# Three buffers instead of four for the transposed unit vectors of a pair of heads, from batch 3 on

## The chip, the core and the metric

The kernel runs on one core of a Trainium2 chip. The metric is device time in microseconds (us) of one execution, the median of several runs. TensorE (PE) does the matrix products, VectorE (DVE) and ScalarE (ACT) move and transform what it leaves in its eight banks, GpSimd (POOL) issues the loads of inputs and weights, SyncE (SP) issues stores and the loads of intermediate results.

## What is computed

Attention with unit queries and keys, followed by a mixer and a two-layer perceptron:

```python
q_n = q / (np.linalg.norm(q, axis=-1, keepdims=True) + 1e-06)
k_n = k / (np.linalg.norm(k, axis=-1, keepdims=True) + 1e-06)
attn = softmax(np.matmul(q_n, k_n.transpose(0, 1, 3, 2)) / tau)
x = np.matmul(attn, v)                 # 8 batches, 12 heads, 448 rows, 64 wide
h = x.transpose(0, 2, 1) @ U @ V       # mixes rows through rank 32
u = x + h.transpose(0, 2, 1)           # 8 x 448 x 768
out = u + np.maximum(u @ w_ch1, 0.0) @ w_ch2     # 768 -> 3072 -> 768
```

## The kernel before

**Two halves that share PE.** Attention goes batch by batch and, in a batch, by six pairs of heads. The perceptron goes over 28 tiles of 128 tokens: a first group of three and one single tile, then twelve groups ("hosts") of two. Hosts 0 to 5 do their first layer at L1299 and their second, in seven products instead of eight, at L1328. Hosts 6 to 11, which run after attention, use seven products for both layers (L1192 and L1328). While attention runs, perceptron products fill PE wherever attention's next step isn't ready.

**Who sets the order.** Everything is first recorded as operations with an engine, a planned duration, dependencies, and slots of buffer rings that it takes and gives back. A planner (`Plan.run`) then walks through planned time and fixes the order of instructions on every engine. An operation that needs a slot is not placed before the planner believes the slot free. Some operations (squares, copies, relus) may go to ACT or DVE, whichever is free first in the plan. On the chip each engine runs its list strictly in order.

**The life of a pair.** The q and k of two pairs are loaded together by POOL (L596). Squares (ACT L657 or DVE L661), their sums (DVE L665), root and inverse (ACT L679 and L680, DVE L685 and L687), and two scalings (DVE L733) give the unit vectors of a pair, `xn`. From batch 2 on eight PE transposes (L574 from `qk_all`, "the flip of the pair") put them into a bank and one copy (ACT L1475 or DVE L1477, `sqk<-bank`) into a tile of the ring `r_qkT`. That tile is what the change is about. The scores of three (pair, key chunk) slots at a time are one burst of matmuls (L797), seven bursts to a batch from batch 2 on. The exponentials are ACT L815, the product with V is L842, its scaling DVE L873 and L874. A tile of `r_qkT` comes free when the last burst that reads its pair is done. Because the last 64 keys of two pairs share a slot, burst 2 reads pairs 1, 2 and 3, and burst 4 reads pairs 3, 4 and 5.

**The ring.** `r_qkT` is a `Shrink`: six tiles for the first 18 pairs (`NPAIR * WHOLE`, three batches), and then only those listed in `left`, in turn. The other tiles' memory passes to the perceptron's weight sums (`T4` at L1107 lies over tiles 0 and 1), once `r_gone2` says that they are free.

**After a batch.** Its result X is projected (L959), expanded again (L1012) and added (DVE L1021). Each token tile of 128 rows is then stored by SP (L1050, `u<-X_sb`, 192 KB), turned by six PE transposes (L574 from `X_sb`), copied back over X in place by ACT L1475 or DVE L1477 (`X_sb<-bank`), and stored turned (L1060). The in-place copy may not start before the L1050 store has read X, so it waits for that store's landing. V of a batch is loaded by POOL with eleven transfers (L619, L624), right behind the batch's last load of q and k in POOL's list.

**The other rings of this path.** `r_xn` holds two pairs from batch 3 on and `r_ld` two loads of two pairs. A pair is scaled only after the flip two pairs earlier, and a load of q and k starts only after the scalings two loads earlier. So a flip that comes later makes the scalings, the loads and the V loads behind them come later.

Of the kernel before, what the change touches and what calls it, by code (L numbers as in the profile page):

```python
# [317 lines left out]
def kernel(  # L318
# [18 lines left out]
    NPAIR = H // 2  # L337
# [14 lines left out]
    WHOLE = 3  # L352
# [21 lines left out]
    def fixed_ring(tiles):  # L374
# [6 lines left out]
            for i in range(3)]  # L381
# [13 lines left out]
    r_inv = ring(4, [SCH, 2, G, SC], FP, "inv")  # L395
    qkT_t = sqk_t[:, 3 * SQ:]
    r_qkT = Shrink([qkT_t[:, 2 * SC * SCH * i:2 * SC * SCH * (i + 1)].rearrange("p (b s) -> p b s", b=2 * SC)
                    for i in range(6)], NPAIR * WHOLE, (2, 3, 4, 5))
    X_t = const.tile([128, 2 * 4 * C], BF, name="X_sb")
    r_X = fixed_ring([X_t[:, 4 * C * i:4 * C * (i + 1)].rearrange("p (t c) -> p t c", t=4) for i in range(2)])  # L400
    A_t = const.tile([128, 3, C], BF, name="A_sb")
# [1288 lines left out]
```

## Time and profile before

| what | value |
|---|---|
| median of 3 runs | 572.73 us (572.58 to 574.4) |
| the profiled execution | 573.77 us, of which its span 572.0 us |
| PE busy | 561.3 us (98%), 6721 matmuls |
| DVE busy | 464.3 us (81%) |
| ACT busy | 306.2 us (54%) |
| POOL busy | 148.5 us (26%) |
| granted PE clock | 1.000 |
| last score burst starts | 381.9 us |

Busy time is a sum over the whole span. The text below reads three more views: windows of ten microseconds, which give each engine's busy time in a stretch; the waits, which say who waited for whom; and the timeline, where a row gives start, length, engine, line, operation, output and input, count, and in brackets the idle time before it with its releaser.

### The profile page before, as it was taken

To read this page: it belongs to the slowest core of one execution; us is meant where nothing else is said; L and a number is where in the kernel's file an instruction comes from. 1 tells how busy PE (TensorE), PEld (TensorE's weight loads), DVE (VectorE), ACT (ScalarE), POOL (GpSimd) and SP (SyncE) were. 2 spreads that over 40 slices of the span, in tenths; PEclk is the share of its full clock that TensorE was granted. 3 is DMA by queue.
4 is the path that set the end of the run, shared out by engine and by line. 5 is a ranking of instruction groups with operands and counts; after the bars stand their busy time and mean duration, and the time that the engine had idled before them with its cause. 6 is when DMAs were issued, how large, how long until landed. Compare 5 with 4: busy or idle time off the path is not lost.

```text
span 572.0 us, 16131 instructions
## 1 busy us (share of the span) xinstructions
PE 561.3 (98%) x6721; PEld 412.7 (72%) x6722; DVE 464.3 (81%) x1061; ACT 306.2 (54%) x495; POOL 148.5 (26%) x180
## 2 busy tenths in 40 slices
PE   8899999999999999999999999999999999999996
PEld 6565656768767758767867766876969696969784
DVE  8979859999898989979969976687897776758583
ACT  7977655766567874766865684560404141414140
POOL 8526241002424225124120510001030303030302
PEclk9999999999999999999999999999999999999999
DMA  9999997632968849349645922312124121221201
GB/s 156 204 207 139 210 192 107 144 84 52 105 155 128 87 88 177 64 93 136 95 83 101 131 70 71 112 30 84 30 78 127 37 83 31 83 69 45 79 7 55
DMA packets 116264, 57.61 MB, mean 101 GB/s; under 512 B 72256, under 2 KB 116192, under 8 KB 116192
## 3 DMA queue, kind: packets, MB, share of 16 engines
q0 software_dynamic: 72352, 25.73, 39.8%
q1 hardware_dynamic: 43840, 30.87, 18.8%
q8 instruction: 52, 0.85, 0.6%
q14 instruction: 20, 0.16, 0.1%
HBM read 61.65 MB, written 20.64 MB: 144 GB/s over the span
## 4 chain that ended last, share of the span: by engine, by line
PE 91%; DVE 5%; ACT 1%; DMA 1%; issue 1%; POOL 0%; SPq 0%; DVEq 0%; POOLq 0%
PE bank L1328 28%; PE bank L1299 16%; PE bank L1192 15%; PE bank L842 8%; PE bank L797 6%; PE bank L1411 6%; PE bank L1453 6%; PE bank L574 5%; DVE qk_all L733 2%; PE bank L1012 1%; DVE ss L665 1%; PE bank L959 1%; DMA relu<-in_k_dram 1%; DVE X_sb L1021 0%; DMA out_dram<-relu 0%
## 5 line engine op out<-in xcount | busy, mean ns | idle before, releaser
L815 ACT ACTIVATE attn<-bank 128x896 bf16<-128x896 f32 (+1 forms) x163 | 140.1, 915 | 35.8 <-PE bank L797 35.3
L1328 PEld LDWEIGHTS <-relu 128*128 128x128 bf16 x1008 | 95.5, 98 | 66.2 <-issue 7.7
L1299 PE MATMUL bank<-uT,w_sb 128*128 128x256 bf16 x864 | 106.1, 273 | 1.6 <-ACT relu L1309 1.4
L1328 PE MATMUL bank<-w_sb,relu 128*128 128x384 bf16 x576 | 103.4, 326 | 0.0
L1299 PEld LDWEIGHTS <-w_sb 128*128 128x128 bf16 x864 | 81.0, 98 | 20.3 <-issue 9.9
L665 DVE TENSOR_REDUCE ss<-sqk 112x8 f32<-112x512 bf16 x95 | 62.1, 675 | 3.1 <-ACT sqk L657 2.6
L733 DVE TENSOR_TENSOR qk_all<-qk_all,inv 112x512 bf16<-112x512 bf16 x93 | 60.5, 683 | 0.3
L842 PE MATMUL bank<-v_nat,attn 128*128 128x65 bf16 (+1 forms) x1536 | 58.3, 193 | 0.8 <-DVE X_sb L880 0.6
L842 PEld LDWEIGHTS <-attn 128*128 128x128 bf16 (+1 forms) x1536 | 53.8, 97 | 5.4 <-issue 3.3
L596 POOL DMA_DIRECT2D qk_all<-in_q_dram x24 | 17.7, 738 | 147.9 <-ACT attn L815 49.1
L1309 ACT ACTIVATE relu<-bank 128x512 bf16<-128x512 f32 x48 | 28.7, 598 | 44.1 <-PE bank L1299 43.3
L1192 PEld LDWEIGHTS <-w_sb 128*128 128x128 bf16 x864 | 49.3, 98 | 0.8
L797 PE MATMUL bank<-sqk 64*64 64x448 bf16 (+1 forms) x460 | 46.9, 356 | 0.7 <-ACT sqk L1475 0.5
L1229 ACT COPY attn<-bank 128x512 f32<-128x512 f32 x18 | 10.6, 587 | 65.6 <-PE bank L1192 60.6
L1220 ACT ACTIVATE relu<-relu 128x512 bf16<-128x512 bf16 x36 | 22.7, 630 | 29.7 <-DVE relu L1214 28.8
L1192 PE MATMUL bank<-uT,w_sb 128*128 128x128 bf16 x648 | 38.1, 219 | 0.0
L1353 POOL TENSOR_TENSOR relu<-relu,u_nat 128x384 f32<-128x384 f32 x7 | 8.4, 1205 | 110.0 <-ACT relu L1351 82.7
L1411 PE MATMUL bank<-uT,w_sb 128*128 128x384 bf16 (+1 forms) x288 | 35.6, 273 | 0.0
L619 POOL DMA_DIRECT2D v_nat<-in_v_dram x42 | 31.1, 746 | 17.2 <-DMA w_sb<-in_moe_w_ch_dram 14.6
L1453 PE MATMUL bank<-w_sb,relu 128*128 128x384 bf16 x192 | 35.4, 326 | 0.0
L874 DVE TENSOR_TENSOR X_sb<-bank,rd 128x256 bf16<-128x256 f32 x72 | 30.6, 425 | 2.6 <-DVE rd L873 0.2
L1353 POOL TENSOR_TENSOR attn<-attn,u_nat 128x384 f32<-128x384 f32 x6 | 12.8, 2156 | 69.0 <-ACT attn L1351 69.0
(137 smaller groups left out, 943.2 us busy)
## 6 DMA issues: line engine op xcount, KB each, us to landing
qk_all<-in_q_dram POOLq DMA_DIRECT2D x23, 224.0 KB, 4.2
qk_all<-in_k_dram POOLq DMA_DIRECT2D x23, 224.0 KB, 5.5
u_nat<-u SPq DMA_DIRECT2D x25, 192.0 KB, 2.5
w_sb<-in_moe_w_ch_dram POOLq DMA_DIRECT2D x4, 1152.0 KB, 17.9
w_sb<-in_moe_w_ch_dram POOLq DMA_DIRECT2D x8, 576.0 KB, 15.5
uT<-uT SPq DMA_DIRECT2D x24, 192.0 KB, 3.0
u<-X_sb SPq DMA_DIRECT2D x22, 192.0 KB, 2.0
uT<-X_sb SPq DMA_DIRECT2D x21, 192.0 KB, 3.1
```

What stands on the lines that cost most here:

```text
L619: ops = [load(lambda j=j, r0=r0, c=c, s0=s0, s1=s1: nc.gpsimd.dma_start(out=v_t[b % 2][r0:r0 + s1 - s0, :, j, 0:D], in_=src[c, s0:s1]), (s ...
L665: lambda i=i, a0=a0, a1=a1, sq=sq: nc.vector.reduce_sum(ss.tile[:, i, a0:a1, :].rearrange("p h c -> p (h c)"), sq.tile[:, 0:a1 - a0, :].re ...
L733: (nc.gpsimd if pool_ else nc.vector).tensor_mul(dst, src, sc)
L797: nc.tensor.matmul(out=out, lhsT=qkT.tile.rearrange("p b s -> p (b s)")[r, n0:n0 + w], rhs=qkT.tile[r, SC:2 * SC, :].rearrange("p c s -> p ...
L815: exps.append(plan.add(Op("ACT", act_t(2 * S, 0.058), lambda sc=sc, c=c, attn=attn: nc.scalar.activation(out=attn.tile[:, :, off:off + S] ...
L842: nc.tensor.matmul(out=av.tile[:, t, 0:D + 1], lhsT=tail.tile[:, hh, 128 * t:128 * (t + 1)] if tail and j == SC - 1 else (attn if j < SC - ...
L874: nc.vector.tensor_mul(X.tile[:, :, h * D:(h + 1) * D], av.tile[:, :, 0:D], rd.tile.to_broadcast([128, 4, D]))
L1192: o = plan.add(Op("PE", pe_t(128), lambda i=i, j=j, jj=jj: nc.tensor.matmul(out=mm.tile[:, 128 * jj:128 * jj + 128], lhsT=left[k](i, j), r ...
L1299: o = plan.add(Op("PE", pe_t(256), lambda j=j, e=e, cc=cc, mm=mm: nc.tensor.matmul(out=mm.tile[:, 256 * e:256 * e + 256], lhsT=w1_sb[:, cc ...
L1328: o = plan.add(Op("PE", pe_t(CH), lambda j=j: nc.tensor.matmul(out=mm.tile[:, 0:CH], lhsT=left[k](j), rhs=right[k](j), start=(first and j ...
L1411: o = plan.add(Op("PE", pe_t(n), lambda cc=cc: nc.tensor.matmul(out=mm.tile[:, m:m + n], lhsT=w1_sb[:, cc, f * 128:(f + 1) * 128], rhs=uT. ...
L1453: nc.tensor.matmul(out=mm.tile[:, 0:c1 - c0], lhsT=relu.tile[:, f, i * 128:(i + 1) * 128], rhs=w2_t[:, f, c0:c1], start=(f == 0), stop=(f ...
```

## The change

The ring of the transposed unit vectors keeps three tiles instead of four after its first 18 pairs:

```diff
     r_qkT = Shrink([qkT_t[:, 2 * SC * SCH * i:2 * SC * SCH * (i + 1)].rearrange("p (b s) -> p b s", b=2 * SC)
-                    for i in range(6)], NPAIR * WHOLE, (2, 3, 4, 5))
+                    for i in range(6)], NPAIR * WHOLE, (3, 4, 5))
```

Pair n now takes over the tile of pair n - 3, where it took that of pair n - 4. Tile 2 joins those that `r_gone2` waits for. No instruction is added or removed; the planner lays all of them out anew with the narrower ring.

## Prediction

> **What bounds the kernel.** I read the page's shares first, then the waits of PE, then windows, then the timeline around the one wait that mattered.
>
> ```profile
> PE 561.3 (98%) x6721; PEld 412.7 (72%) x6722; DVE 464.3 (81%) x1061; ACT 306.2 (54%) x495; POOL 148.5 (26%) x180
> ...
> PE 91%; DVE 5%; ACT 1%; DMA 1%; issue 1%; POOL 0%; SPq 0%; DVEq 0%; POOLq 0%
> ```
>
> PE is the bound: 98% busy, 91% of the chain of waits. From 30 to 560 us the windows of ten microseconds show it at 9.8 to 10.0, with one exception, 8.62 between 320 and 330. The waits of PE from 25 to 400 us are 2.6 us in all, and the longest is
>
> ```profile
> PE bank L1299 <- ACT relu L1309: 1.4, 1, 1.4
> ```
>
> (us in total, times, longest). So the change can gain little more than these 2.6 us, 0.45% of the time, and can lose whatever new waits it makes. Is that one wait touched? The timeline of the four engines around it:
>
> ```profile
> 315.75 0.70 POOL L596 DMA_DIRECT2D qk_all<-in_q_dram  x1 [14.69 <-ACT relu L1309]
> ...
> 317.14 4.43 POOL L619 DMA_DIRECT2D v_nat<-in_v_dram  x6
> ...
> 321.56 0.33 SPq L1050 DMA_DIRECT2D u<-X_sb  x1
> ...
> 328.59 0.80 ACT L1475 COPY X_sb<-bank 128x768 bf16<-128x768 bf16 x1 [3.40 <-PE bank L1299]
> 329.29 0.60 ACT L1309 ACTIVATE relu<-bank 128x512 bf16<-128x512 f32 x1
> ...
> 329.94 0.31 PEld L1299 LDWEIGHTS <-w_sb 128*128 128x128 bf16 x3 [1.56 <-issue]
> ```
>
> The releaser named for the copy at 328.59 had long been done. The entry for its line shows ACT's sequencer held before it, and the entry for the store of 321.56 shows why:
>
> ```profile
> L1475 ACTq EVENT_SEMAPHORE  x1: 5512/5512/5512, 323.0 to 323.0; - x1
> ```
> ```profile
> DMA to landing us min/median/max: 7.0/7.0/7.0
> ```
>
> That store took 7.0 us to land where the median of all L1050 is 2.1, because it was issued among the V loads of batch 7. The in-place copy waited for it, the relu behind the copy waited, and PE ran out of banks. From the store's issue to PE's restart are 329.94 - 321.56 = 8.38 us; PE lost 1.56.
>
> **The change, part by part.** *The ring itself* removes no work: both programs have the same number of PE rows, and the order of the two, compared engine by engine, is identical up to the flip of batch 3's fourth pair (near 155 us). The wider `r_gone2` costs nothing: the sums that lie over tiles 0 and 1 (L1117 into `sqk`, 124 us) stand before that point, unmoved. *Flips* move back by one burst: pair 5 of batches 3 to 7 is flipped after burst 3 instead of burst 2, and most others likewise. The shortest cover left between a flip and the burst that reads it is that of batch 3's pair 3: 15 L1328 and some transposes, about 2.8 us, against a copy of 0.62 (DVE) or 0.91 us (ACT). Elsewhere a product with V (32 L842) lies between as well. Cost 0; without that cover it would be about 1 us each. *End of attention*: the last product with V stands 9 matmuls earlier than before, among filler; from host 6 on PE is busy without a break in both. Cost 0.
>
> *POOL's queue.* A later flip makes the scaling (L733) two pairs on later, this the load of q and k, and this the V loads behind it in POOL's list. In the new order the three V runs for batches 5, 6 and 7 stand 150, 160 and 85 matmuls later. Against SP's stores this means:
> - The stores of tile 5 (batches 3 and 5) now precede the load of q by 10 matmuls or more, at least one L733 (0.68 us). Such a place exists before: the store of 314.62, 1.1 us ahead of the load at 315.75, landed in 1.9. So the 1.56 us wait **goes: -1.56**, and behind it nothing else is late: ACT's next L815 follow from bursts that PE itself starts. The store of tile 3 of batch 4 has one L733 between it and its q load too: 0.
> - Site A, about 240 us: the store of tile 6 of batch 3 now lies inside the V run for batch 5, about 5.4 us behind its q load (before: 5.8 behind), and its copy is on ACT with an L1309 behind it.
> - Site B, about 335 us: the same for tile 6 of batch 5, about 6.6 us behind the q load of the V run for batch 7.
>
> What each costs: PE's own time from the store to the matmul that needs the relu, by the timeline (17 L1299 in 1.87 us, 0.11 each; a burst 0.77 with its switch; flip 0.40; L842 0.03 each; X flip 0.34). A: 8 L1299 0.88 + burst 0.77 + 17 L1299 1.87 + flip 0.40 + 32 L842 0.96 + X flip 0.34 + 16 L1299 1.76 = 6.98. B has 7 and 15 L1299: 6.76. With the row's 8.38 us, A waits 8.38 - 6.98 = **1.40** and B 1.62. B's store comes later in the run, though: all V loads had landed at 329.4, 13.6 us behind the q load, so B may see less; a latency of 6.1 gives 0.8. I take **1.2** (0.8 to 1.6). Queued behind each copy on ACT: one L1309, then the three L815 of the next burst, which PE needs only some 20 matmuls later.
>
> Here the Trainium skill reads otherwise. "DMA: Bandwidth & Descriptors", section on the anatomy of one DMA, prices a transfer at 2.0 us plus bytes over 436e3 per us: 2.45 us for 192 KB. With that the copies at A and B find their store landed (the transposes end 4.4 us after it), both cost nothing, and the sum is -1.56. The row says 7.0 in a V run and 1.9 to 2.1 outside it. I follow the row, since both new sites are inside a run[...].
>
> *Banks after burst 3 of batch 4* (site C, near 222 us). In the new order an X flip follows directly on this burst; a L1299 four matmuls later takes the bank that DVE's in-place copy frees. DVE stands before that copy with L874, L1346, L1021, L685, L687, twice L733: 0.43 + 0.56 + 0.55 + 0.17 + 0.35 + 1.37 = 3.4 us, plus 0.17 (L873) and the copy 0.5, so 4.1 against PE's 3.9. The wait is 0.2 if DVE comes to it on time and 1.3 if it is a microsecond late, as its load just before allows (from burst 2 to burst 3 the new order holds 12.6 us of DVE work beside 11.6 of PE, each instruction at its row's mean). **0.7** (0 to 1.3).
>
> **Sum:** -1.56 + 1.40 + 1.2 + 0.7 = +1.7 us. The profiled execution (span 572.0, 1.8 around it, 573.8) would become 575.5; it lies 1.0 above the median shown, so the median becomes 572.73 + 1.74 = **574.5**.
>
> **Rivals.** *R1, the stores land in time.* If issue to landing stays under 5.5 us at A and B, they cost nothing, C closes, and the old wait is gone: 572.73 - 1.56 = **571.2**, faster. For it: stores at 317.65 and 319.92 in the same run landed in 6.0 and 4.6, so it isn't always 7. Against: six L1050 stores inside the V runs near 217 and 265 us belong to the same kind of traffic, and the maximum of the line is 7.0. It decides at 5.5 us.
>
> *R2, DVE becomes the bound.* The planner gives DVE 9 more squares (0.417), 3 relus (0.688), 2 `A_sb` copies and one `X_sb` copy (0.55), and 2 `sqk` copies (0.616) fewer: 3.75 + 2.06 + 1.65 - 1.23 = 6.2 us more, and ACT 7.4 less. DVE's rests before are
>
> ```profile
> 240.00:250.00 10.00, 10.00 (x109) 6.49 (x108) 5.73 (x15) 7.18 (x10) 2.66 (x3) 1.00 0.33 61
> 290.00:300.00 10.00, 10.00 (x103) 5.91 (x102) 4.57 (x12) 6.71 (x10) 3.03 (x4) 1.00 0.25 61
> ```
>
> (the fifth figure: 5.73 and 4.57 us of ten). In the new order the stretches between bursts 6 and 0 hold 4.3 us of DVE work where 2.4 stood (batch 4) and 5.5 where 1.1 stood (batch 5), beside some 4 to 5 us of PE. DVE would reach the next relus (L1311) late. If half of the 6.2 us ends in PE waits, with the collisions at 1.0 net: 572.73 + 3.1 + 1.0 = **576.8**. Against: DVE was 95% or more busy in several windows before, and PE waited for it 0.8 us in all from 25 to 400 us.
>
> *R3, one wait for another.* A takes the place of the old wait, B and C hide: 572.73 - 1.56 + 1.4 = **572.6**. For it: the waits near 217 and 265 us before, with stores as late, cost PE nothing since filler was there.
>
> That the ring isn't full, so that nothing moves, is excluded: the flips move.
>
> **Chances.** What a measurement of this kernel tells from no change is about 0.3%, 1.7 us. The forecast has 0.40 (its own range 573.4 to 575.8, 0.6 of it beyond the bound), R1 0.15 (two thirds of it faster by more than the bound, if small waits of PE go too), R2 0.25, R3 0.20. Slower: 0.24 + 0.25 + 0.01 = 0.50; faster 0.11; same 0.39. Half of R1 and the upper part of R2 stay outside the range: 571.5 to 577.3.
>
> **What would show it.** Right: no wait of PE near 328 us; two waits of PE for ACT's L1309, 1 to 1.6 us, near 240 and 335, each with an in-place X copy ahead of it whose store took 6 to 7 us; one of 0.2 to 1.3 for DVE's L1477 near 222. R1: L1050 at no more than about 5 us in the runs, and no such waits. R2: PE waits for L1311 or `sqk` copies of DVE, DVE near 10 of 10 at 240 to 250 and 290 to 300 with no late store. Wrong altogether: a PE wait at a burst (L797) for a flip's copy, or a longer stretch after 400 us, where I expect the same 174 us.

## The result and the profile after

The changed kernel takes **572.38 us** in the median of 20 runs (571.77 to 573.37), the kernel before, run beside it, 573.81 (572.58 to 574.97). The ratio is 0.9977 with a 95% interval of 0.9969 to 0.9984: about 1.3 us faster (1.43 between the medians), where 1.7 slower was forecast. The forecast started from a median of three runs, 572.73; beside the changed kernel that kernel's median is 1.1 higher, so what follows compares differences and not the 574.5 with the 572.38. The profiled execution takes 571.8 us, its span 570.0 (before: 573.8 and 572.0).

The page's shares of busy time and of the chain of waits, of the kernel after:

```profile
PE 559.8 (98%) x6721; PEld 411.9 (72%) x6722; DVE 469.4 (82%) x1074; ACT 300.9 (53%) x482; POOL 148.8 (26%) x180
...
PE 92%; DVE 3%; DMA 2%; POOL 1%; issue 1%; ACT 0%; DVEq 0%; POOLq 0%; ACTq 0%
```

DVE has 13 instructions and 5.1 us more, ACT 13 and 5.3 us fewer: the count is the prediction's, the times are below its 6.2 and 7.4. PE is the bound as before. The waits of PE from 25 to 400 us, after:

```profile
PE bank L842 <- DVE X_sb L880: 0.6, 2, 0.4
PE bank L1328 <- ACT relu L1309: 0.3, 1, 0.3
PE bank L1012 <- issue: 0.2, 1, 0.2
```

The wait of 1.4 us before L1299 is gone. In its place stands one of 0.3 before L1328. It is site B of the prediction, at 333.5 us. The timeline there:

```profile
327.05 0.32 SPq L1050 DMA_DIRECT2D u<-X_sb  x1
...
332.71 0.80 ACT L1475 COPY X_sb<-bank 128x768 bf16<-128x768 bf16 x1 [0.91 <-DMA u<-X_sb]
333.40 1.09 ACT L1309 ACTIVATE relu<-bank 128x512 bf16<-128x512 f32 x2
...
334.06 0.32 PE L1328 MATMUL bank<-w_sb,relu 128*128 128x384 bf16 x1 [0.25 <-ACT relu L1309]
```

The bracket of the copy now names the store itself. Store, copy, relu, matmul: this is the forecast chain with a shorter first link, since the store landed at 332.64, after 5.59 us. Site A, at 236 us:

```profile
227.06 0.70 POOL L596 DMA_DIRECT2D qk_all<-in_q_dram  x1 [18.21 <-ACT relu L1309]
...
231.74 0.32 SPq L1050 DMA_DIRECT2D u<-X_sb  x1
...
236.57 0.80 ACT L1475 COPY X_sb<-bank 128x768 bf16<-128x768 bf16 x1 [1.17 <-PE bank L842]
237.32 0.60 ACT L1309 ACTIVATE relu<-bank 128x512 bf16<-128x512 f32 x1
```
```profile
DMA to landing us min/median/max: 4.8/4.8/4.8
```

The store is issued 4.7 us behind the load of q, the copy does wait for its landing at 236.50 and the relu follows at once, but PE hasn't come to need it. The cost is 0. Site C is in the same trace, 2 us earlier than expected:

```profile
218.79 1.29 DVE L733 TENSOR_TENSOR qk_all<-qk_all,inv 112x512 bf16<-112x512 bf16 x2
218.99 0.74 PE L797 MATMUL bank<-sqk 64*128 64x448 bf16 x6
...
219.67 0.51 PE L574 MATMUL bank<-ident,X_sb 128*128 128x128 bf16 x6
...
220.27 0.36 DVE L1477 COPY X_sb<-bank 128x384 bf16<-128x384 bf16 x1 [0.18 <-issue]
```

DVE was through its two L733 when the X flip ended, so it came on time, and the starts of two L1299 at 220.3 lie 0.23 us further apart than they should: the lower value of the prediction's two (0.2, and 1.3 for a late DVE).

Small waits do not all appear in the list. So I also took the distance between the starts of consecutive matmuls and subtracted the median distance of their shape; bursts and projections aside, where the same distances stand in both, places above 0.12 us from 120 to 400 us are:

| place | before | after |
|---|---|---|
| old wait, 328 us | 1.55 | - |
| site A, B, C | - | 0, 0.42, 0.23 |
| load of `uT` (L908), 173 us | 0.19 | - |
| small ones of before (162.9, 216.4, 231.2, 316.9, 368.7 us) | 1.12 | - |
| small one of after (222.6 us) | - | 0.26 |
| sum | 2.86 | 0.91 |

The difference, 1.95 us, is the 2.0 by which the spans differ. Three fifths are the old wait less B; the rest is small waits, of which the prediction treated only C. The small ones are no accident of one execution: taken in the same way, those of before come to 1.10 to 1.12 us in each of its three profiled executions, and C and the one of after to 0.23 and 0.26 in each of its four.

### The profile page after: what moved, and what is told of

It is laid out like the page before. It is cut to its first block, busy times and chain, and to the rows that moved or that the text cites. A ratio compares the mean times of both kernels' runs of the same rounds, so it can differ in the third digit from the quotient of the medians.

```text
span 570.0 us, 16134 instructions
## 1 busy us (share of the span) xinstructions
PE 559.8 (98%) x6721; PEld 411.9 (72%) x6722; DVE 469.4 (82%) x1074; ACT 300.9 (53%) x482; POOL 148.8 (26%) x180
## 4 chain that ended last, share of the span: by engine, by line
PE 92%; DVE 3%; DMA 2%; POOL 1%; issue 1%; ACT 0%; DVEq 0%; POOLq 0%; ACTq 0%
PE bank L1328 29%; PE bank L1299 16%; PE bank L1192 15%; PE bank L842 8%; PE bank L797 6%; PE bank L1411 6%; PE bank L1453 6%; PE bank L574 4%; PE bank L1012 2%; DMA qk_all<-in_k_dram 1%; DMA u<-X_sb 1%; DVE qk_all L733 1%; PE bank L959 1%; DVE ss L665 1%; POOL qk_all L596 0%
## 5 line engine op out<-in xcount | busy, mean ns | idle before, releaser
L1328 PEld LDWEIGHTS <-relu 128*128 128x128 bf16 x1008 | 95.5, 98 | 65.0 <-issue 6.7
L1299 PE MATMUL bank<-uT,w_sb 128*128 128x256 bf16 x864 | 104.5, 273 | 0.1
L1328 PE MATMUL bank<-w_sb,relu 128*128 128x384 bf16 x576 | 103.7, 326 | 0.3 <-ACT relu L1309 0.3
L1299 PEld LDWEIGHTS <-w_sb 128*128 128x128 bf16 x864 | 81.4, 98 | 18.6 <-issue 8.6
L733 DVE TENSOR_TENSOR qk_all<-qk_all,inv 112x512 bf16<-112x512 bf16 x93 | 60.8, 681 | 0.2
L1309 ACT ACTIVATE relu<-bank 128x512 bf16<-128x512 f32 x45 | 26.8, 597 | 47.6 <-PE bank L1299 46.6
L1353 POOL TENSOR_TENSOR relu<-relu,u_nat 128x384 f32<-128x384 f32 x7 | 9.0, 1289 | 92.8 <-ACT relu L1351 66.3
L1353 POOL TENSOR_TENSOR attn<-attn,u_nat 128x384 f32<-128x384 f32 x6 | 12.8, 2154 | 69.1 <-ACT attn L1351 69.1
```

The lines of the kernel that those rows point to most:

```text
L733: (nc.gpsimd if pool_ else nc.vector).tensor_mul(dst, src, sc)
L1299: o = plan.add(Op("PE", pe_t(256), lambda j=j, e=e, cc=cc, mm=mm: nc.tensor.matmul(out=mm.tile[:, 256 * e:256 * e + 256], lhsT=w1_sb[:, cc ...
L1328: o = plan.add(Op("PE", pe_t(CH), lambda j=j: nc.tensor.matmul(out=mm.tile[:, 0:CH], lhsT=left[k](j), rhs=right[k](j), start=(first and j ...
```

## The experiments

Theories on record: **T1**, the gain is the in-place copy that no longer waits for a late store; **T2**, it is the squares, relus and copies that went from ACT to DVE; **T3**, it is PE's other order. Within T1, on what makes a store in a V run late: **N**, the number of 192 KB stores in flight; **V**, the V loads alone. Ratios are to the kernel before run on the same chip.

### Taking the V loads away

```diff
     order = plan.run()
+    for o in got[7, 0, "v"]:
+        o.fn = lambda: None
```

Before, without the V loads of batch 7:

> The kernel before without the eleven V loads of batch 7 (left out of the computation: batch 7's products use V of batch 5, which is still in that buffer); nothing else moves. T1 (the late landing of the store of 321.56 inside that V run makes the wait of 1.56 us): the store lands in 1.9 to 2.6 us, the copy (L1475) and the relu behind it start when their banks are ready, no PE wait near 328 us, time -1.5 us (ratio 0.9973). T2 (the changed kernel gains from the squares, relus and copies that went from ACT to DVE): the store may land early but the PE wait near 328 stays at 1 us or more, time same within 0.4 us. T3 (the gain comes from some other order of PE's filler): as T2.

After, without them:

> The changed kernel without the eleven V loads of batch 7 (left out of the computation: batch 7's products use V of batch 5); nothing else moves. T1: the store of tile 6 of batch 5 lands in 1.9 to 2.6 us instead of 5.6, the 0.4 us wait of PE near 333 us goes, time -0.4 us against the changed kernel, so -1.7 against before (ratio 0.9970). Rival (that 0.4 us is ordinary bank traffic of L1309): it stays, no change against the changed kernel.

Measured: 0.9986 (0.9976 to 0.9996), 0.8 us faster, and 0.9971 (0.9959 to 0.9982). In before's order the store takes 3.52 us instead of 6.96. ACT around it:

```profile
322.04 0.33 SPq L1050 DMA_DIRECT2D u<-X_sb  x1
...
326.36 0.80 ACT L1475 COPY X_sb<-bank 128x768 bf16<-128x768 bf16 x1 [0.70 <-PE bank L574]
327.75 0.60 ACT L1309 ACTIVATE relu<-bank 128x512 bf16<-128x512 f32 x1 [0.59 <-PE bank L1299]
```

The copy starts 4.3 us behind the store instead of 7.0, and the relu now waits for its own bank: PE is no longer the one that is kept. Matmul by matmul, PE gains 1.55 us at this one place and next to nothing elsewhere. In the new order the store takes 1.99 us and the 0.42 us at B goes. T1 holds at both places; T2 and T3 do not explain the old wait. Two things expected for the first were missed. The time gained is half of the 1.5 us (more executions of before, further down, put the old wait at 1.2 in the mean, which the interval allows). And the latency is 3.52 where 1.9 to 2.6 was expected. N, the stores ahead, explains that only in part: of the two turned stores before it one had landed and the other did so 0.33 us after its issue; the rest is open.

### The number of stores ahead

In before's order, two turned stores (tiles 3 and 4 of batch 5) go behind the L1050 store:

```diff
     order = plan.run()
+    behind = made_t[2, 5][0].deps[0]
+    for o in (made_t[2, 3][1], made_t[2, 4][0]):
+        order.remove(o)
+        order.insert(order.index(behind) + 1, o)
+        behind = o
```

> The kernel before with the turned stores (L1060) of tiles 3 and 4 of batch 5 moved in SP's order from ahead of the L1050 store of tile 5 to behind it (and behind its in-place copy). The V run of batch 7 stays. Theory N (what made 7.0 us is the number of 192 KB stores in flight in the V run: two ahead of this one before, one or none at the sites of the changed kernel): the L1050 store takes 4.5 to 5.6 us instead of 7.0, PE's wait near 328 falls from 1.56 to 0.4 or less, time -1.2 to -1.5 us. Theory V (the V loads alone set the landing, whatever stores are ahead; the sites of the changed kernel were earlier or later in the run): latency stays at 6.5 to 7.0, wait 1.2 to 1.6, time same within 0.4 us. T2: time same.

In the new order, the same two stores are issued a second time ahead of site B's store:

```diff
     order = plan.run()
+    place = order.index(made_t[2, 5][0]) + 1
+    for o in (made_t[2, 4][0], made_t[2, 3][1]):
+        order.insert(place, Op("SP", 0.1, o.fn))
+        order[place].start, order[place].by = order[place - 1].start, "SP"
```

> The changed kernel with the turned stores of tiles 4 and 3 of batch 5 issued a second time, just ahead of the L1050 store of tile 6 in the V run of batch 7 (384 KB more written, with the same contents). Theory N: that store takes 7 us or more instead of 5.6, PE's wait near 333 grows from 0.4 to 1.5 us or more, time +1.1 to +2 us against the changed kernel, so no better than before. Theory V: latency within 0.5 us of 5.6, wait 0.3 to 0.8, time same as the changed kernel (ratio to before 0.9977).

Measured: 0.9990 (0.9978 to 1.0002), latency 5.16 us and no wait at 328, so the wait did what was expected, while the time, 0.6 us less, fell short of the 1.2 to 1.5 and its interval takes in no change; and 0.9999 (0.9989 to 1.0010), latency 7.01, wait 1.87 by the starts. The list of waits and the store's own entry, new order with two more stores:

```profile
PE bank L1328 <- ACT relu L1309: 1.7, 1, 1.7
```
```profile
DMA to landing us min/median/max: 7.0/7.0/7.0
```

This is the forecast for B: with a latency of 7.0 the wait is there, and it takes the whole gain away. So the mechanism and the place were right, and whether the change gains anything hung on the latency. V falls at B, by one execution with three stores ahead. In before's order the effect is only a tendency, as more executions show below.

### Half the ring at a time

```diff
-        return m % len(self.tiles) if m < self.until else self.left[(m - self.until) % len(self.left)]
+        return m % len(self.tiles) if m < self.until else (x := getattr(self, "late", self.left) if m >= 30 else self.left)[(m - self.until) % len(x)]
...
-                    for i in range(6)], NPAIR * WHOLE, (2, 3, 4, 5))
+                    for i in range(6)], NPAIR * WHOLE, (2, 3, 4, 5)); r_qkT.late = (3, 4, 5)
```

Pair 30 is the first of batch 5. Four tiles first, then three:

> Half of the change: four tiles for batches 3 and 4, three only from batch 5 on. The order returns to that of before up to batch 5 and moves the V run of batch 7 behind all stores of batch 5. T1 (the only thing that matters is which stores lie in a V run with an in-place copy and a relu behind it): the wait near 328 goes and no store of batch 5 lands late, PE's waits from 25 to 400 us at most 1.1 us, time at or below the changed kernel's: -1.3 to -1.8 us (ratio 0.9968 to 0.9977). T2 (the squares, relus and copies that go from ACT to DVE bring it, about half of them before batch 5): -0.3 to -0.8.

Three first, then four (the two lists exchanged):

> The other half of the change: three tiles for batches 3 and 4, four from batch 5 on. Around batch 5 the stores, the V run of batch 7 and the copy on ACT stand against one another as before. T1: the store of tile 5 of batch 5 lands in 5.5 to 7 us inside the V run, PE waits 0.3 to 1.6 us for L1309 behind its copy near 328 us (by how many turned stores are ahead of it: with two, 1.2 or more), and the time is within 0.8 us of before (ratio 0.9986 to 1.0010). T2: half of the gain, -0.3 to -0.8 us, with or without that wait.

The second stayed within what T1 says: 0.9991 (0.9982 to 1.0000), latency 5.80, a wait of 0.40 at 328 us and none at 173. But two turned stores were in flight ahead of that store, for which 1.2 or more was expected, and the time, 0.5 us less, suits T2 as well. The first was a **miss**: the wait at 328 is gone, yet it took 1.0044 (1.0023 to 1.0065), with runs from 573.9 to 579.6 us. Its profiled execution has one long wait of PE:

```profile
PE bank L1299 <- DMA uT<-uT: 1.1, 1, 1.1
```

This is a second collision, which the prediction did not have: the load of `uT` (L908) for the perceptron's next host, issued by SP at 168.33 us behind POOL's loads of q and k, took 6.45 us. Before has it too, smaller. Its timeline, before:

```profile
166.25 0.73 POOL L596 DMA_DIRECT2D qk_all<-in_q_dram  x1 [7.34 <-DVE qk_all L733]
166.97 0.70 POOL L596 DMA_DIRECT2D qk_all<-in_k_dram  x1
167.93 0.57 SPq L908 DMA_DIRECT2D uT<-uT  x1
...
173.31 0.44 PEld L1299 LDWEIGHTS <-w_sb 128*128 128x128 bf16 x5 [0.41 <-DMA uT<-uT]
```

and after:

```profile
167.37 0.57 SPq L908 DMA_DIRECT2D uT<-uT  x1
168.32 0.72 POOL L596 DMA_DIRECT2D qk_all<-in_q_dram  x1 [9.85 <-DVE qk_all L733]
169.04 0.70 POOL L596 DMA_DIRECT2D qk_all<-in_k_dram  x1
```

The later flip moves POOL's loads behind the load of `uT`, which lands in 2.9 us instead of 5.3. Here the same shift of POOL's queue that made A and B took a collision away.

To see what else varied, the kernel ran again:

> The kernel with four tiles up to batch 4 and three from batch 5 on, once more, for a second profile: its runs lay between 573.9 and 579.6 us while its profiled execution, with the wait at 328 gone and 1.3 us at 173, was at the low end. Something in it varies by up to 6 us. If it is the load of uT at 173 us (T1 extended), a slow execution shows that wait at 2 us or more; if it is another place, the profile of a slow execution shows which; median again 575 to 576.

Measured: 574.35 us (572.4 to 576.6), 1.0009 (0.9992 to 1.0025). The median expected (575 to 576) was missed, and the profiled execution lies in the middle of the runs, so what the longest of them lose it can't show. The load of `uT` took 5.25 us with a wait of about 0.1, so it isn't what this one loses; its long waits, by the starts 1.47 and 0.70 us, are at 296 to 298 us:

```profile
PE bank L1328 <- DVE relu L1346: 1.3, 1, 1.3
PE bank L842 <- ACT attn L815: 0.5, 1, 0.5
```

L1346 stands in DVE's list behind two squares and their sums. DVE and POOL there:

```profile
292.34 3.73 DVE L661 TENSOR_TENSOR sqk<-qk_all 112x512 bf16<-112x512 bf16 x2
```
```profile
292.78 0.93 POOL L1353 TENSOR_TENSOR relu<-relu,u_nat 128x384 f32<-128x384 f32 x1
293.66 1.79 POOL L1353 TENSOR_TENSOR O_sb<-relu,u_nat 128x384 f32<-128x384 f32 x2
```

The first of the two squares took 3.40 us, where the other took 0.41, and ended 0.3 us after the third sum of POOL (L1353). In the first execution of the same kernel DVE's three squares near there took 0.42 each. So one square cost this execution some 2 us; what held it is open (see the last section), and whether the runs above 577 us are more of the same no profile shows.

### The balance of DVE and ACT

```diff
     order = plan.run()
+    moved = [1680, 1716, 1744, 1746, 1750, 2075, 2077, 2079, 2109, 2111, 2113, 2143, 2474, 2476, 2508, 2542, 2546, 2873, 2911, 2913, 2941]
+    for o in order:
+        if o.seq in moved:
+            o.by = "DVE" if o.by == "ACT" else "ACT"
```

> Before's order, but 21 squares run on the engine that the changed kernel gives them (15 from ACT to DVE, 6 from DVE to ACT): the part of the new balance of DVE and ACT that can be had without the new order. T1: the wait near 328 stays at 1.2 to 1.6 us, time within 0.4 us of before, or slower by what DVE is later. T2: -0.5 to -1.3 us.

Measured: 1.0033 (1.0020 to 1.0046), 1.9 us **slower**, with the wait at 328 still 1.55, those at 173 and 217 us larger than before's (0.45 and 0.43, where 0.19 and 0.32 stood) and a new one of 0.58 at 224. T2 falls for the squares: in before's order they cost time. In the new order, where the relus and copies moved too, DVE has room for them. Windows of ten microseconds, after (PE, PEld, DVE, ACT, POOL):

```profile
240.00:250.00 10.00, 10.00 (x110) 6.46 (x108) 8.36 (x20) 6.66 (x12) 2.94 (x4) 1.00 0.54 87
290.00:300.00 10.00, 10.00 (x112) 6.08 (x110) 6.55 (x17) 6.42 (x11) 2.66 (x3) 1.00 0.71 128
```

DVE has gone from 5.73 to 8.36 and from 4.57 to 6.55, with PE at 10.00 in both.

### The copy behind the relu

```diff
     order = plan.run()
+    copy = made_t[2, 5][0].deps[0]
+    i = order.index(copy)
+    j = next(n for n in range(i, len(order)) if order[n].by == "ACT" and order[n].eng == "ACT/DVE" and order[n] is not copy)
+    order.insert(j + 1, copy)
+    del order[i]
```

> Before's order, but the in-place copy (L1475) of tile 5 of batch 5 stands one relu (L1309) later in ACT's list; the store of 321.56 and the V run stay. T1: the store still lands in 6.5 to 7 us, but the relu no longer stands behind it, so the wait of 1.56 goes; what follows may wait for the bank that the copy frees later, 0 to 0.6 us; time -0.9 to -1.5 us by the trace, about half of that or more in the medians. Rival (PE waits for banks that relus alone fill): the wait stays at 1.2 us or more.

In this kernel the turned store of the tile goes out ahead of the copy and writes the tile unturned. Measured: 0.9994 (0.9983 to 1.0005). In the trace the store still takes 5.89 us (6.5 to 7 were expected), which would have cost 0.48 (see below), and nothing is lost at 328; the 0.61 us at 173 us hides part of the gain. The relu behind the copy was the link to PE, as T1 has it; by time alone the run tells nothing.

### Mending both places in before's order, and site B after

The load of `uT` ahead of two output stores:

```diff
     order = plan.run()
+    sp = [o for o in order if o.by == "SP"]
+    load = [o for o in sp if o.fn.__code__.co_firstlineno == 908][3]
+    ahead = sp[sp.index(load) - 2]
+    order.remove(load)
+    order.insert(order.index(ahead), load)
```

> Before's order, but SP's load of uT (L908, 167.9 us) stands ahead of the two output stores (L1093) that precede it, so it is issued before POOL's load of q of 166.25 us instead of 1.7 us behind it. T1 extended (a second collision, at 173 us, that the prediction missed: the load of uT took 5.3 us and 4.9 to 6.5 us in the variants with before's order, PE waited 0.2 to 1.3 us for it, and 2.9 to 3.3 us with no wait where the new order issues it ahead of the load of q): it lands in 2.3 to 3.5 us, no PE wait at 173, the wait of 1.56 at 328 stays; time -0.3 to -0.7 us (ratio 0.9988 to 0.9995), and the runs lie closer together than before's (572.3 to 575.5). Rival: that wait is a bank's or the trace's noise; time same, spread as before.

The same, with the two turned stores moved as above:

> Before's order with both moves on SP alone: the load of uT ahead of two output stores, and the turned stores of tiles 3 and 4 of batch 5 behind the L1050 store of tile 5. Nothing on PE, ACT, DVE or POOL moves. T1 extended: no PE wait of 0.3 us or more at 173 or 328, time -1.5 to -2.0 us by the profile, ratio 0.9966 to 0.9977, as the changed kernel or better. Rival (the changed kernel's gain needs its new order or its balance of DVE and ACT): ratio 0.9985 or more.

In the new order, the turned store of tile 5 behind site B's store:

```diff
     order = plan.run()
+    turned_5 = made_t[2, 5][0]
+    order.remove(turned_5)
+    order.insert(order.index(made_t[2, 6][0].deps[0]) + 1, turned_5)
```

> The changed kernel with the turned store (L1060) of tile 5 of batch 5 moved behind the L1050 store of tile 6 in SP's order. Theory N: the L1050 store has no store of 192 KB ahead of it and takes 4.2 to 5.2 us instead of 5.6; PE's wait near 333 falls from 0.42 to 0 to 0.1; time -0.3 to -0.4 us against the changed kernel, ratio to before 0.9968 to 0.9974. Rival: latency as before, same time as the changed kernel.

Measured: 0.9997 (0.9986 to 1.0007); 0.9986 (0.9975 to 0.9998); 0.9961 (0.9947 to 0.9976). The load of `uT` issued at 165.66 us lands in 2.78 us, and the 0.19 us at 173 goes; that is too little to see in the time, and the spread (573.3 to 574.3) is narrower. With both moves the gain is 0.8 us, less than expected, and the ratio is one that the rival named (0.9985 or more). The trace says where the rest is: the store still took 5.97 us and PE waited 0.56; the small waits of before's order stay, as nothing on PE moved; and a wait of 0.86 stands at 447 us, where before had none (0.87 with the first move alone):

```profile
PE bank L1328 <- DVE relu L1272: 0.7, 1, 0.7
```

There DVE meets POOL's sums in another way than before (see the last section). So SP's order alone gives part of what the change gained, not all. The third has no wait above 0.2 us at 333 and the lowest median measured here.

### Do latency and wait vary by themselves?

> The kernel before, once more, for a second profiled execution. If the landing of the store near 321 us varies from run to run (5.9 to 7.0 us in variants with this order there) and PE waits for what is above 5.4 us, this execution shows a wait of 0.5 to 1.6 us at 328, equal to its latency less 5.4 within 0.1; and 0.2 to 0.6 us at 173 for the load of uT. Rival (latency fixed by the order): 7.0 and 1.56 again.

> As for the second profiled execution of the kernel before: wait at 328 equal to latency less 5.4 us, latency between 5.9 and 7.0.

> The changed kernel, once more, for a second profiled execution. The store of tile 6 of batch 5 lands in 5.0 to 6.1 us, PE waits for what is above 5.15 us (0 to 0.9); the store of tile 6 of batch 3 lands in 4.3 to 5.5 us with no wait of PE; no wait at 173.

> As for the second profiled execution of the changed kernel: waits of PE at 333 equal to latency less 5.15 us (0 to 0.9), none at 240 and 173.

The lists of waits: second execution of before,

```profile
PE bank L1299 <- ACT relu L1309: 1.0, 1, 1.0
```

third of before,

```profile
PE bank L1299 <- ACT relu L1309: 0.8, 1, 0.8
```

second of after:

```profile
PE bank L1328 <- ACT relu L1309: 0.5, 1, 0.5
```

With every execution that has the site, to a hundredth of a us (latency from the store's issue to its last semaphore update in the trace, wait by the starts of the matmuls):

| old site: latency / wait | site B: latency / wait |
|---|---|
| before 6.96 / 1.55, 6.54 / 1.12, 6.38 / 0.98 | after 5.59 / 0.42, 5.88 / 0.71, 5.61 / 0.43, 6.06 / 0.88 |
| other squares 6.89 / 1.55 | two more stores 7.01 / 1.87 |
| load ahead 6.35 / 0.94 | turned store later 5.00 / 0, 5.25 / below 0.12 |
| three then four 5.80 / 0.40 | no V loads 1.99 / 0 |
| both moves 5.97 / 0.56 | |
| turned later 5.16 / 0, no V loads 3.52 / 0 | |

Where there is a wait, latency less wait is 5.34 to 5.42 at the old site and 5.14 to 5.18 at B, whatever was edited: **PE waits for what the landing takes beyond a fixed cover**, which is PE's own work in between. The load of `uT` at 173 us behaves alike: in eight executions where PE waited for it (0.10 to 1.30 us), latency less wait is 5.15 to 5.16. The same order gives 6.4 to 7.0 in three executions, so the row of 7.0 was the high end of what it was taken for. The table also corrects N. At B the groups are apart (5.0 to 5.3 with no turned store ahead, 5.6 to 6.1 with one, 7.0 with three); in before's order two stores ahead gave 5.8 to 7.0 and none 5.2 and 6.0, which overlap. Nor does it hold for the six other L1050 stores that before issued in V runs, near 217 and 265 us: 4.64 and 6.51 with no store ahead, 6.32 and 6.76 with one, 6.41 and 6.76 with two. What sets the latency within a V run is open.

Last, the changed kernel and its variant side by side:

> The changed kernel, timed beside the next one on one chip: ratio to before 0.9969 to 0.9984 again; PE's wait near 333 us 0.3 to 0.9.

> The changed kernel with the turned store of tile 5 of batch 5 behind the L1050 store of tile 6, once more, beside the changed kernel on one chip: no wait of PE at 333, latency of that store 4.5 to 5.2 us, 0.3 to 0.7 us faster than the changed kernel (what its wait at 333 is in the mean). Rival: the first timing (0.9961) was the chip's, and the two are the same within 0.2 us.

Measured: 572.43 us, 0.9979 (0.9971 to 0.9988), with 0.88 at B; and 572.12, 0.9974 (0.9963 to 0.9985), with none. The wait is gone in the trace, the 0.3 us between the medians lies within the intervals.

## Why the prediction was wrong

- **Old wait, -1.56: right in cause and place.** Without the V loads, with fewer stores ahead, and with the copy behind the relu it goes, and in the changed kernel it went since tile 5's stores landed in 1.84 us ahead of the V runs. The size was at the high end: 1.2 us in the mean of three executions of before.
- **"With the row's 8.38 us, A waits 1.40": the step that failed.** The chain and the cover were right. PE's work of 6.98 us less the 1.42 from landing to restart is a cover of 5.56 at A, and 6.76 less 1.42 is 5.34 at B (measured: 5.17). The latency wasn't: 4.76 at A (4.76 to 5.05 in six executions of the changed kernel and its variant) and 5.59 at B. By the prediction's own formula A costs 0 and B 0.25 (measured: 0.42), not 2.6 together. One row, the maximum of its line, was taken for a property of the V run, though the two turned stores in that run had landed in 6.0 and 4.6 and though the point from which the wait decides, 5.5 us, lay between. It was chosen because it was the row of the same kind of store; that row had two turned stores in flight ahead of it, A and B had one. But a better choice of row would hardly have saved the forecast: the six other rows of that kind in before's V runs, which the prediction named without their latencies, are the 4.64 to 6.76 above, and their median of 6.46 still prices A at 0.9 and B at 1.1. Taken as a range, 4.64 to 6.96, they price A at 0 to 1.4 and B at 0 to 1.6, which leaves the sign of the sum open. The sign came from this step: with the measured latencies the prediction's own sum is -1.56 + 0 + 0.25 + 0.7 = -0.6.
- **The rule set against it** (2.45 us for 192 KB) was too low by 2.3 to 3.1 us at the two sites, but on the right side of the cover at A. The Trainium skill's section gives that fit for transfers that GpSimd issues, which the prediction doesn't say; these stores are SP's, and away from POOL's loads those of before took 1.9 to 2.1.
- **Site C, 0.7:** it was there at 0.23, the lower end, as DVE was on time.
- **What was left out, -1.05 net:** the wait for the load of `uT` at 173 us (0.19), gone by the same shift of POOL's loads behind SP's transfers, and the small waits of 0.12 to 0.34 us (1.12), which the new order took away and nearly didn't replace (0.26). The prediction named 2.6 us of waits and then priced only one of them. No experiment isolates these small ones; they are read from the traces, and which part of the new order removes each is open.
- **R1 came nearest, in part by luck.** It forecast 1.56 us less, and 1.43 was measured. Its reason holds at A; at B the store landed in 5.59, above its 5.5, and C didn't close. What these two cost, the small waits that it didn't count gave back. R2 was refuted in the new order, though the cost of the squares is real in before's (1.9 us). R3 had the right form, one wait for another, but at B and at less than half of the size.

The corrected sum for the profiled execution: -1.56 + 0 + 0.42 + 0.23, and -0.19 - 1.12 + 0.26 for the small waits, is -1.96; the spans differ by 2.0. The forecast for it was +1.7: of the 3.7 between, A and B are 2.2, the small waits 1.05 and C 0.5. In the mean of the executions the old wait is 1.2 and B's 0.6 (four executions), so -1.2 + 0.6 + 0.23 - 1.05 = -1.4, against -1.43 between the medians.

## What to carry to other kernels

Price a wait as latency less cover: the cover is the waiting engine's own work in between and can be counted to 0.2 us, while the latency of a transfer that shares its stretch with others is a range. Where the cover lies inside that range, price the wait as a range from the whole set of rows, not from the largest; if the sign of the sum then stays open, say so. And when a change moves one queue against another, go through every transfer of both on the stretch, loads as well as stores, since the shift that makes one collision undoes another.

## What was not expected of the hardware

In the kernels before and after, an L1050 store took 1.8 to 2.2 us away from POOL's loads (but for one of 3.8, near 372 us after, with none near) and 4.6 to 7.0 inside V runs (but for two at their ends, 2.0 and 2.7). V loads aren't needed for it: four such stores near 103 us, beside loads of q and k and one another, took 5.6 to 7.0 in these two, where the prediction has 1.9 to 2.1 outside a V run. At the two sites the V loads were the larger part of it (6.96 to 3.52 without them in before's order, 5.59 to 1.99 after).

By the rows, DVE and POOL hold each other up, and either may lose. In before, near 445 us, DVE's products of 128x512 run at 0.42 us each while POOL's three sums take 5.72, the first of them 3.65. With the load of `uT` ahead it is the other way round: the sums take 3.03 (one alone 0.91), and three of DVE's products 1.13 each; the last of these is the one that PE waits for at 447 us.

```profile
444.83 3.03 POOL L1353 TENSOR_TENSOR attn<-attn,u_nat 128x384 f32<-128x384 f32 x3 [25.05 <-ACT attn L1351]
444.90 1.14 DVE L1271 TENSOR_TENSOR relu<-relu 128x512 bf16<-128x512 bf16 x1
445.96 1.13 DVE L1273 TENSOR_TENSOR relu<-relu 128x512 bf16<-128x512 bf16 x1
447.01 1.13 DVE L1272 TENSOR_TENSOR relu<-relu 128x512 bf16<-128x512 bf16 x1
```

The Trainium skill, "SBUF — State Buffer", section on who interferes with whom, says that GpSimd and VectorE share a port pair under an exclusive lock, and that a VectorE instruction with two inputs in SBUF contends with a GpSimd instruction that reads SBUF. These rows agree; no run here isolates it.

The square of 3.40 us ended just after POOL's last sum, which fits as well. But at its usual 0.42 us it would have been over at 292.76, before the first sum began at 292.78, and in the same kernel's other execution, with the squares at 293.84 us and the sums at 294.28, they took 0.42 each. What held the one square the trace doesn't explain.
